# Spreading the roundings of weight sums, a later free time for five buffers, and separate banks for the last product

## The chip, the cores and the metric

The kernel runs on one core of one Trainium2 chip. The metric is the device time of one launch in microseconds (us), as the median of several runs; lower is better. A core has TensorE (PE, matmuls), VectorE (DVE), ScalarE (ACT), GpSimd (POOL) and SyncE (SP); here SP issues nearly all DMA transfers.

## The reference

Sigmoid attention, then a feed-forward layer with squared ReLU:

```python
S = q.shape[2]                                   # q, k, v: (8, 12, 448, 64)
scores = np.matmul(q, k.transpose(0, 1, 3, 2)) / np.sqrt(64) - np.log(S)
attn = np.matmul(1.0 / (1.0 + np.exp(-scores)), v)
x = attn.transpose(0, 2, 1, 3).reshape(3584, 768)
h = x @ w_in                                     # (768, 2048)
r = np.maximum(h, 0.0)
out = (s * (r * r) + b) @ w_out                  # (2048, 768)
```

All in float32. The kernel keeps the precision by splitting a float32 operand into a high part (rounded to the matmul format fp32r) and a low part (the difference), and by three matmuls for each product: high by high, high by low, low by high (`PARTS`).

## The kernel before

**Attention (0 to 246 us of the trace).** 8 batches by 12 heads are done in 24 steps, "quads" of four heads. In each step TensorE makes the scores (L812, L833) and the product with v (L845, L853), ScalarE the sigmoid (L788), VectorE the split of q and k. What these engines have left goes to the weights of the feed-forward layer. `convert` turns a block of stored weights into the form that is needed (integer and float steps on VectorE and ScalarE, L659 to L677), `sums_out` (L913) makes sums and differences of blocks of the second weight matrix for the fast scheme below. A group g of sums is made (`make`, VectorE), its high part is rounded (`hi`, ScalarE, L930), its low part is a subtraction on VectorE (`lo`), and SP stores it to DRAM. In which step each of the three is done stands in the table `SUMS_AT`: for f = 0 and 1 three rows, for `make`, `hi` and `lo`, with seven groups each. `at_step` puts a function into a step's list of an engine.

**Plain stage (246 to 371 us).** The first 512 tokens go through the two matrices in the ordinary way, in 16 blocks of the 2048 inner columns: `ffn1` (L981) fills a PSUM bank ph_f, ScalarE empties it into r_f (L1505) and makes g_f from it, VectorE makes the low part of g_f, and `ffn2` (L1374) multiplies it into po. The weights w_l_f of matrix l, block f, are split here: high part on ScalarE (`base_hi`, L694), low part on VectorE (`base_lo`, L638 by `sub`).

**Fast scheme (371 to 972 us).** The other 3072 tokens, in two groups of three blocks of 512, use a scheme that multiplies sums of blocks (`LAYERS`). One layer has 29 products, each in two halves p of 12 matmuls of 512 columns, 0.22 us apart. Layer 0 makes h from operands s, layer 1 the output from operands g. An operand of product r in layer 0 of group n is s`n`_`r`_0h (high part, ScalarE L1145) and s`n`_`r`_0l (low part, VectorE L638). Weight sums wu come by DMA from DRAM. During layer 0 of the first group `later_sums` (L1286) makes the last weight sums t_*: VectorE adds, ScalarE rounds (L1348), VectorE subtracts (low part), SP stores to DRAM (L1354) and then the buffer is free again.

**The order of the work.** From the plain stage on, all work is first listed as operations with an engine, a cost, a due time and what they need. `Flow.run` (L227) then simulates the engines and fixes, engine by engine, the order in which they are written out. An operation can also need a buffer. Buffers are kept by `Slots` (L561), a list sorted by the time since when each is free; `tile` takes the first of that list, `free` puts one back with the planner's time. `cx.more(t2, 5, "t")` (L1061) adds five buffers that lie over the attention's memory. The planner's start time of an operation is not before its buffer's free time:

```python
def more(self, pl, n, tag, old=None):
    self.free_ += [(pl, f"{tag}{i}", old(i) if old else 0.0) for i in range(n)]
    self.free_.sort(key=lambda x: x[2])
...
key = (max(at, o.ready, o.heap.ready(need)), o.due)
```

The order within an engine is fixed once it is written; where an instruction uses a buffer whose last reader is on another engine or in a DMA, it waits for that one on the chip.

**The end.** `build` (L430) lists the products. The last product (number 20 of layer 1 in the second group) writes three parts of an output block into banks of its second half, and `last_out` adds them to C1_20, which goes out in three stores.

## Time and profile before

| | us |
|---|---|
| median of 3 runs | 977.67 |
| lowest, highest | 976.95, 978.43 |
| the profiled execution | 977.93 |
| its span in the trace | 976.1 |
| TensorE busy in it | 970.9 |
| VectorE busy | 875.8 |
| ScalarE busy | 719.8 |

All times of the trace count from the start of the span. An instruction's row gives its start and duration; on VectorE and ScalarE successive rows overlap by a little under 0.1 us. Idle time before an instruction stands in brackets with what ended it. TensorE's granted clock was 1.00 over the span.

### The profile page before, as it was taken

What the parts mean: (1) busy time and instruction counts of PE and PEld (TensorE: products, weight loads), DVE (VectorE), ACT (ScalarE), POOL (GpSimd) and SP (SyncE); (2) the same over time, 40 slices, a digit from 0 to 9 for tenths busy, and PEclk for the clock granted to TensorE, in tenths of its full rate; (3) what the DMA queues carried; (4) which work ended last, traced back from release to release, by engine and by line L of the source; (5) the groups of instructions that cost most, each with busy time, mean ns of one, the idle gap of its engine ahead of it and who ended that gap; (6) DMA issues with size and microseconds to landing.
All of it is one profiled execution on the core that took longest, in us unless ns stands there. A gap on an engine that the chain in (4) does not pass through costs nothing.

```text
span 976.1 us, 13892 instructions
## 1 busy us (share of the span) xinstructions
PE 970.9 (99%) x5192; PEld 764.8 (78%) x5192; DVE 875.8 (90%) x995; ACT 719.8 (74%) x807; POOL 0.2 (0%) x4
## 2 busy tenths in 40 slices
PE   9999999999999999999999999999999999999998
PEld 4555545555788888888888888888888888888887
DVE  5998999999899988899999999999787649999995
ACT  7999999999777767557799996333457499995330
POOL 0000000000000000000000000000000000000000
PEclk9999999999999999999999999999999999999999
DMA  8789999998569999989986666799866666666675
GB/s 327 286 308 350 326 364 401 351 396 311 191 263 365 354 403 413 414 279 320 341 287 206 202 203 205 226 333 330 311 201 202 207 200 207 200 205 202 201 251 194
DMA packets 97377, 276.68 MB, mean 283 GB/s; under 512 B 10016, under 2 KB 23456, under 8 KB 97312
## 3 DMA queue, kind: packets, MB, share of 16 engines
q1 hardware_dynamic: 97024, 275.35, 81.2%
q8 instruction: 41, 0.67, 0.3%
q10 hardware_dynamic: 288, 0.46, 0.1%
q14 instruction: 24, 0.20, 0.1%
HBM read 193.99 MB, written 81.79 MB: 283 GB/s over the span
## 4 chain that ended last, share of the span: by engine, by line
PE 97%; ACT 1%; DVE 1%; issue 0%; DMA 0%; DVEq 0%; ACTq 0%
PE o L1166 30%; PE h L1166 27%; PE pav L845 11%; PE psc L812 7%; PE po L1374 6%; PE ph L981 6%; PE e L1166 4%; PE psc_l L833 2%; PE pav L853 2%; PE pav L812 1%; DVE C L635 0%; ACT a L788 0%; PE idle L873 0%; DMA xd<-xo 0%; ACT w L694 0%
## 5 line engine op out<-in xcount | busy, mean ns | idle before, releaser
L1166 PE MATMUL h<-s_0h,wu 128*128 128x512 f32 x800 | 239.2, 379 | 0.0
L1166 PEld LDWEIGHTS h<-s_0h,wu 128*128 128x128 f32 x800 | 151.2, 189 | 21.5
L1166 PE MATMUL h<-s_0l,wu 128*128 128x512 f32 x400 | 151.6, 379 | 0.0
L1166 PE MATMUL o<-g_0h,wu 128*128 128x512 f32 x464 | 147.5, 379 | 0.0
L1166 PE MATMUL o<-g_1h,wu 128*128 128x512 f32 x456 | 144.9, 379 | 0.0
L788 ACT ACTIVATE a<-psc,nls 128x896 f32<-128x896 f32 x120 | 113.7, 1027 | 10.4 <-PE psc L812 8.3
L845 PE MATMUL pav<-a,v 128*64 128x448 f32 x576 | 113.8, 543 | 0.0
L1166 PEld LDWEIGHTS o<-g_0h,wu 128*128 128x128 f32 x464 | 87.7, 189 | 12.4
L1166 PEld LDWEIGHTS o<-g_1h,wu 128*128 128x128 f32 x456 | 86.2, 189 | 12.2
L845 PEld LDWEIGHTS pav<-a,v 128*64 128x64 f32 x576 | 39.1, 137 | 62.7 <-issue 56.0
L1166 PE MATMUL o<-g_0l,wu 128*128 128x512 f32 x232 | 87.9, 379 | 0.0
L1166 PE MATMUL o<-g_1l,wu 128*128 128x512 f32 x228 | 86.4, 379 | 0.0
L1166 PEld LDWEIGHTS h<-s_0l,wu 128*128 128x128 f32 x400 | 75.6, 189 | 10.7
L1258 ACT ACTIVATE G<-G 128x1024 f32<-128x1024 f32 x56 | 57.7, 1049 | 27.2 <-DVE G L638 13.6
L1374 PE MATMUL po<-g,w 128*128 128x512 f32 x288 | 64.4, 379 | 0.0
L1374 PEld LDWEIGHTS po<-g,w 128*128 128x128 f32 x288 | 54.4, 189 | 7.7
L981 PE MATMUL ph<-x0h,w 128*128 128x512 f32 x192 | 59.8, 380 | 0.3 <-ACT r L1505 0.3
L1128 ACT COPY G<-h 128x1024 f32<-128x1024 f32 x36 | 36.0, 1013 | 29.1 <-PE h L1166 28.3
L638 DVE TENSOR_TENSOR qkl<-qk,qkh 128x1664 fp32r<-128x1664 f32 (+3 forms) x26 | 44.9, 1726 | 13.9 <-ACT qkh L767 13.6
L1258 ACT ACTIVATE G<-G,b_sb,s_sb 128x1024 f32<-128x1024 f32 x40 | 49.0, 1235 | 0.1
L1166 PEld LDWEIGHTS o<-g_0l,wu 128*128 128x128 f32 x232 | 43.8, 189 | 6.2
L1166 PEld LDWEIGHTS o<-g_1l,wu 128*128 128x128 f32 x228 | 43.1, 189 | 6.1
(195 smaller groups left out, 1908.0 us busy)
## 6 DMA issues: line engine op xcount, KB each, us to landing
wu<-wd SPq DMA_DIRECT2D x232, 512.0 KB, 4.4
wd<-t SPq DMA_DIRECT2D x42, 768.0 KB, 7.5
qk<-qk_t SPq DMA_DIRECT2D x23, 896.0 KB, 7.4
st<-w_out SPq DMA_DIRECT2D x16, 768.0 KB, 8.8
st<-w_in SPq DMA_DIRECT2D x16, 768.0 KB, 9.2
v<-v_t SPq DMA_DIRECT2D x24, 448.0 KB, 5.7
xd<-xo SPq DMA_DIRECT2D x24, 448.0 KB, 4.3
out_t<-C SPq DMA_DIRECT2D x17, 512.0 KB, 5.0
```

The costliest lines, as they stand in the source:

```text
L638: nc.vector.tensor_tensor(o, x, y, op=ALU.subtract)
L788: nc.scalar.activation(a, psc[:, :, :S], AF.Sigmoid, bias=nls, scale=SCALE)
L812: nc.tensor.matmul(o[j][:, :S], two[wi][r, i, cols], paired(two[xi][r, i, :S]), start=m == 0, stop=m == 2,)
L833: nc.tensor.matmul(spread(psc[half[i], j, :S]), x[r, i, 1, 3 * P :], x[r, i, 0, :], start=True, stop=True,)
L845: nc.tensor.matmul(pav[i][r, :S], ld_[1][:, 3 * i + c, j, :], a[i, c][:, j, :], start=c == 0, stop=False,)
L853: nc.tensor.matmul(pav[i][r, :S], ld_[1][half[i], 6, j, :], a[half[i], j, :], start=False, stop=True,)
L981: nc.tensor.matmul(ph, w[:, k, wi, kc * P : (kc + 1) * P], paired(x0[h][xi][:, cc, :]), start=m == 0, stop=m == 3 * NCC - 1,)
L1128: nc.scalar.copy(o, self.view(x, l))
L1166: nc.tensor.matmul(bank.t[0][:, j], wt[:, w, wi, x * P : (x + 1) * P], paired((o.hi, o.lo)[xi][:, c, :]), start=new and m == 0, stop=stop ...
L1258: v.by = flow.op("ACT", cost, lambda: nc.scalar.activation(f32(v.t), f32(v.t), *a, **kw), (v.by,))
L1374: nc.tensor.matmul(pos[e], w[:, k, wi, kc * P : (kc + 1) * P], paired(g[:, gi, :]), start=first and i == 0, stop=last and i == 2,)
```

## The change

Three edits.

1. `SUMS_AT` and `sums_out`: a step has at most one rounding of sums on ScalarE. Before, steps 11, 16 and 21 had two. Three of the 14 roundings go to VectorE as a cast (steps 10, 18 and 20, written as negative numbers); one low part moves from step 18 to 19; the last sum of one group moves from step 5 to 6.
2. The five t2 buffers count as free at 5.0 of the planner's time, not 0.0. The planner's decisions in the plain stage and in layer 0 of the first group come out otherwise, from that stage on.
3. The last product uses the banks of the two lanes that are not busy with the product before it; the addition of an earlier partial result to C1_20 is listed by itself and can run before the last product. Its first half runs 6 matmuls of 512 columns and 12 of 256 in place of 12 of 512.

```diff
--- before.py
+++ after.py
@@ -41,8 +41,8 @@
 PIECES = (2, 1, 1, 2, 1, 1, 2, 1, 1, 2, 1, 1, 2, 1, 1, 2, 1, 1, 2, 1, 2, 1)
 LATE, LATE_AT, LATE_FOR = 2, 2, 5
 SUMS_AT = (
-    ((3, 4, 5, 7, 8, 9, 11), (4, 5, 7, 8, 10, 11, 11), (6, 6, 9, 9, 11, 12, 13)),
-    ((12, 14, 15, 16, 17, 19, 21), (14, 16, 16, 17, 19, 21, 21), (15, 17, 18, 18, 21, 22, 22)),
+    ((3, 4, (5, 5, 5, 5, 6), 7, 8, 9, 11), (4, 5, 7, 8, -10, 10, 11), (6, 6, 9, 9, 11, 12, 13)),
+    ((12, 14, 15, 16, 17, 19, 21), (14, 16, -18, 17, 19, -20, 21), (15, 17, 19, 18, 21, 22, 22)),
 )
 
 
@@ -476,17 +476,20 @@
                     tag = 2 * lane + p if l == 0 else lane
                     new = r in fresh and (l == 0 or p == 0)
                     if l == 0 or p == 0:
-                        bank = Bank(tag, l, None if new else last[tag])
-                        waits = last[tag].readers if tag in last else []
+                        b_was = last.get(tag)
+                        bank = Bank(tag, l, None if new else b_was)
+                        waits = b_was.readers if b_was else []
                         last[tag] = bank
                     else:
                         bank, waits = last[tag], []
                     stop = l == 0 or p == np_ - 1
-                    final_unit = l and end and x == len(seq) - 1 and p == np_ - 1
-                    if final_unit:
-                        part = net.join(*rest[0], Val(u, 1, bank), s_last, f"C{n}_e", True)
+                    final_unit = l and end and x == len(seq) - 1
+                    if final_unit and p == 0:
+                        assert not new and seq[-2][1] != lane
+                        part = net.join(*rest[0], Val(b_was.by, 1, b_was), s_last, f"C{n}_e", True)
                         part.name = k_last
-                        waits = [q for t, b in last.items() if t != tag for q in b.readers]
+                        tags = sorted((t for t in last if t != seq[-2][1]), key=lambda t: t == tag)
+                        waits = [q for t in tags for q in (b_was if t == tag else last[t]).readers]
 
                     ended = None
                     seeds = r in L["seeds"] and not (l and end and x == len(seq) - 1)
@@ -500,7 +503,7 @@
 
                     def fn(n=n, l=l, r=r, p=p, o=o, bank=bank, new=new, stop=stop, final_unit=final_unit):
                         if final_unit:
-                            em.last(n, r, p, o, bank.tag)
+                            em.last(n, r, p, o, tags, p == 0, stop)
                         else:
                             em.unit(n, l, r, p, o, bank, new, stop)
                         o.uses -= 1
@@ -509,8 +512,9 @@
                             flow.heap.free(o.lo)
 
                     u = em.matmuls(flow, net.UNIT, fn, [o.by, *waits], n, l, r, p)
-                    if final_unit:
+                    if final_unit and stop:
                         flow.op("DVE", 2.0, lambda: em.last_out(n, part, s_last), (u, part.by))
+                    bank.by = u
                     if stop and ended:
                         v = Val(u, 1, bank)
                         if l == 0:
@@ -926,8 +930,8 @@
             at[n] = f32(ts[g][:, k, here])
             op(at[n], get(x), sign, get(y))
 
-        def hi(g):
-            nc.scalar.copy(ts[g][:, :, 0], f32(ts[g][:, :, 1]))
+        def hi(g, copy=nc.scalar.copy):
+            copy(ts[g][:, :, 0], f32(ts[g][:, :, 1]))
 
         def lo(g):
             t = ts[g]
@@ -948,9 +952,13 @@
         made_at = collections.Counter()
         for g, (n, h, low) in enumerate(zip(*steps)):
             for i in range(len(SUMS[g])):
-                at_step(n, "DVE", 3.05 + 0.1 * made_at[n] if n > 3 else 4, lambda g=g, i=i: make(g, i))
-                made_at[n] += 1
-            at_step(h, "ACT", 2, lambda g=g: hi(g))
+                m = n[i] if isinstance(n, tuple) else n
+                at_step(m, "DVE", 3.05 + 0.1 * made_at[m] if m > 3 else 4, lambda g=g, i=i: make(g, i))
+                made_at[m] += 1
+            if h > 0:
+                at_step(h, "ACT", 2, lambda g=g: hi(g))
+            else:
+                at_step(-h, "DVE", 3.3, lambda g=g: hi(g, nc.vector.tensor_copy))
             at_step(low, "DVE", 3.25, lambda g=g: lo(g))
 
     pieces = [(l, f + h * (NF // 4)) for f in range(NF // 4) for l in (1, 0) for h in (0, 2, 1, 3)]
@@ -1058,7 +1066,7 @@
     rt, p2, gp = Slots(rt_pool, 2, "r"), Slots(p2_pool, 3, "w"), Slots(gp_pool, 3, "g")
     ps_o = pool(blk_ps, "ps_o", 1, space=PSUM)
     t2 = pool(blk, "t2", 1)
-    cx.more(t2, 5, "t")
+    cx.more(t2, 5, "t", lambda i: 5.0)
     wfp_late = pool(blk, "wfp_late", 1)
     for _, f in late:
         wf_tile(0, f, wfp_late)
@@ -1171,21 +1179,22 @@
                         )
                         m += 1
 
-        def last(self, n, r, p, o, busy):
+        def last(self, n, r, p, o, tags, new, stop):
             wt = fetched[stream.index((n, 1, r, p))]
-            tags = [x for x in range(4) if x != busy]
-            self.ends = []
-            for e, tk in LAST:
-                b = ps.tile([P, 2, TB], F32, tag=f"b{tags.pop(0)}", name=f"o_{e}_{tk.start}")[:, 0, tk]
+            if new:
+                self.ends = [
+                    ps.tile([P, 2, TB], F32, tag=f"b{t}", name=f"o_{e}_{tk.start}")[:, 0, tk]
+                    for t, (e, tk) in zip(tags, LAST)
+                ]
+            for (e, tk), b in zip(LAST, self.ends):
                 q = 0
                 for f in range(2):
                     for wi, gi in PARTS:
                         nc.tensor.matmul(
                             b, wt[:, f, wi, e * P : (e + 1) * P], paired((o.hi, o.lo)[gi][:, f, tk]),
-                            start=q == 0, stop=q == 5, skip_group_check=True,
+                            start=new and q == 0, stop=stop and q == 5, skip_group_check=True,
                         )
                         q += 1
-                self.ends.append(b)
 
         def last_out(self, n, part, sign):
             m, k = self.block[part.name]
```

Most of what moves follows from the second edit and can't be seen in the diff. Rows are in program order of an engine; what stands behind "waits" are the semaphores of the engine (or DMA ring) that the instruction waits for. The change's lines are 4 to 9 higher for the same code (L642 is L638 before).

First place: VectorE at the start of the plain stage. Names are w_l_f for weights (matrix l, block f), wf_f and st_f for a weight block that `convert` still works on and the load that it comes from. Before:

```order
L638 TENSOR_TENSOR w_0_1_2773<-wf_0_1_101,w_0_1_2773 128x3x256 [waits DMAHW2_49,DMAHW6_49,DMAHW1_49,Activation_49]
L638 TENSOR_TENSOR w_1_0_2775<-wf_1_0_96,w_1_0_2775 128x3x256 [waits Activation_49]
L638 TENSOR_TENSOR w_0_9_2778<-wf_0_9_103,w_0_9_2778 128x3x256 [waits Activation_49]
L638 TENSOR_TENSOR w_1_8_2802<-wf_1_8_98,w_1_8_2802 128x3x256 [waits Activation_49]
L659 TENSOR_SCALAR wf_0_7_2740<-st_0_7_2769 128x768 [waits DMAHW7_49]
L659 TENSOR_SCALAR wf_0_15_2741<-st_0_15_2771 128x768 [waits DMAHW0_49]
```

With the change:

```order
L642 TENSOR_TENSOR w_0_8_2748<-wf_0_8_99,w_0_8_2748 128x3x256 [waits Activation_49]
L642 TENSOR_TENSOR w_1_0_2773<-wf_1_0_96,w_1_0_2773 128x3x256 [waits Activation_49]
L663 TENSOR_SCALAR wf_0_7_2740<-st_0_7_2769 128x768 [waits DMAHW7_49]
L642 TENSOR_TENSOR w_0_1_2778<-wf_0_1_101,w_0_1_2778 128x3x256 [waits DMAHW5_49,Activation_49]
L642 TENSOR_TENSOR t_0_0_0_2807<-wf_0_4_113,wf_0_12_115 128x256 [waits DMAHW2_49,DMAHW1_49]
L642 TENSOR_TENSOR w_0_9_2804<-wf_0_9_103,w_0_9_2804 128x3x256 [waits DMAHW6_49,DMAHW2_49,Activation_49]
```

The integer step on wf_0_7, which waits for the load of st_0_7 (DMAHW7), stood behind the low parts of w_0_1, w_1_0, w_0_9 and w_1_8, and stands now ahead of those of w_0_1, w_0_9 and w_1_8. TensorE's next block, ph_1, uses w_0_1.

Second place: VectorE in layer 0 of the first group, where TensorE does products 21, 19 and 1. s0_19_0l is the low part of product 19's operand; t_t4, t_t6, t_t11, t_t13 are weight sums; G00_13 and G01_13 are joins of results. Before:

```order
L638 TENSOR_TENSOR t_t13_4326<-t_t13_4326 128x2x256 [waits DVE_49,Activation_49]
L638 TENSOR_TENSOR t_t4_4432<-wr_4_4025,t_t4_4432 128x2x256 [waits DVE_49]
L638 TENSOR_TENSOR s0_19_0l_4454<-a_0_01_3901,s0_19_0h_4403 128x1024 [waits Activation_49]
L635 TENSOR_TENSOR t_t6_4470<-wr_5_3999,t_t4_4432 128x2x256 [waits DVE_49,PE_49]
L638 TENSOR_TENSOR t_t3_4345<-t_t3_4345 128x2x256
L635 TENSOR_TENSOR t_t11_4477<-wr_4_4025,t_t6_4470 128x2x256 [waits DVE_49]
L638 TENSOR_TENSOR t_t4_4432<-t_t4_4432 128x2x256 [waits Activation_49]
L635 TENSOR_TENSOR a0_t7_4307<-a_0_00_4068,a0_t7_4307 128x1024
L638 TENSOR_TENSOR G00_13_4203<-G00_13_4203,h_0_13_0_4214 128x1024 [waits PE_49]
L638 TENSOR_TENSOR t_o26_4503<-t_t8_4412,t_t11_4477 128x2x256 [waits DVE_49,PE_49]
L638 TENSOR_TENSOR s0_1_0l_4521<-a_0_02_4071,s0_1_0h_4499 128x1024 [waits DMAHW6_49,Activation_49]
```

With the change:

```order
L642 TENSOR_TENSOR t_t13_4327<-t_t13_4327 128x2x256 [waits DVE_49,Activation_49]
L642 TENSOR_TENSOR t_t4_4445<-wr_4_4023,t_t4_4445 128x2x256 [waits DVE_49]
L642 TENSOR_TENSOR a_0_02_4071<-a_0_02_4071,a_0_12_3572 128x1024
L639 TENSOR_TENSOR t_t6_4470<-wr_5_3997,t_t4_4445 128x2x256 [waits DVE_49,PE_49]
L642 TENSOR_TENSOR t_t3_4347<-t_t3_4347 128x2x256 [waits Activation_49]
L639 TENSOR_TENSOR a0_t7_4308<-a_0_00_4068,a0_t7_4308 128x1024
L642 TENSOR_TENSOR G00_13_4202<-G00_13_4202,h_0_13_0_4212 128x1024 [waits Activation_49]
L642 TENSOR_TENSOR t_t4_4445<-t_t4_4445 128x2x256 [waits DVE_49]
L639 TENSOR_TENSOR t_t11_4498<-wr_4_4023,t_t6_4470 128x2x256 [waits PE_49]
L642 TENSOR_TENSOR G01_13_4231<-G01_13_4231,h_0_13_1_4236 128x1024 [waits Activation_49]
L642 TENSOR_TENSOR s0_19_0l_4511<-a_0_01_3901,s0_19_0h_4401 128x1024 [waits DMAHW0_49,DVE_49]
L642 TENSOR_TENSOR t_o26_4514<-t_t8_4425,t_t11_4498 128x2x256 [waits DVE_49]
```

s0_19_0l was two rows behind the low part of t_t13 and waited for ScalarE alone. It is now three rows behind the low part of t_t4 and waits for a DMA (DMAHW0): the store of t_t4 to DRAM, whose buffer it takes. G00_13 ahead of it waits for a copy by ScalarE. The low part s0_1_0l, eight rows behind s0_19_0l before and now seven (outside these rows), waits with the change for TensorE's end of product 19, from which it takes a buffer, and before for a store's landing.

Third place: the rows of ScalarE that the second place waits for, with the change:

```order
L1357 CAST t_t6_4470<-t_t6_4470 128x2x256 [waits DVE_49]
L1136 COPY G00_12_4493<-h_0_13_0_4212 128x1024 [waits DMAHW4_49,PE_49]
L1267 ACTIVATE G00_t1_4123<-G00_t1_4123,b_sb_79,s_sb_78 128x1024 [waits Activation_49]
L1136 COPY G01_12_4501<-h_0_13_1_4236 128x1024 [waits PE_49]
L1155 ACTIVATE s0_24_0h_4506<-a_0_21_3611 128x1024 [waits DMAHW6_49,DVE_49]
```

G00_12 waits for the landing of the store of t_t13 (DMAHW4), whose buffer it takes, and for TensorE.

## Rows read from the trace of the kernel before

**Rows 1.** The page, part 1: engine, busy us, share of the span, instructions.

```profile
PE 970.9 (99%) x5192; PEld 764.8 (78%) x5192; DVE 875.8 (90%) x995; ACT 719.8 (74%) x807; POOL 0.2 (0%) x4
```

**Rows 2.** TensorE's waits over the whole program: us in total, times, longest.

```profile
PE ph L981 <- ACT r L1505: 0.3, 1, 0.3
```

**Rows 3.** Windows of three quads: us, busy by engine, clock, DMA share.

```profile
66.11:76.28 10.17, 10.17 (x81) 5.39 (x78) 9.13 (x12) 9.59 (x12) 0.00 (x0) 1.00 0.88 289
126.21:136.41 10.20, 10.20 (x81) 5.31 (x78) 9.90 (x16) 10.20 (x13) 0.00 (x0) 1.00 1.01 396
206.50:216.50 10.00, 10.00 (x80) 5.39 (x76) 8.97 (x12) 9.59 (x12) 0.00 (x0) 1.00 1.04 407
```

**Rows 4.** Timeline of ScalarE, 120 to 127 us: start, duration, engine, line, operation.

```profile
124.97 1.59 ACT L930 CAST t<-t 128x768 fp32r<-128x768 f32 x2
126.43 1.04 ACT L788 ACTIVATE a_l<-psc_l,nls 128x896 f32<-128x896 f32 x1
```

**Rows 5.** Timeline of VectorE at 240.5 us: a cast of 128x768.

```profile
240.53 0.94 DVE L694 CAST w<-wf 128x768 fp32r<-128x768 f32 x1
```

**Rows 6.** Timeline of ScalarE, 246 to 256 us.

```profile
250.71 3.03 ACT L694 CAST w<-wf 128x768 fp32r<-128x768 f32 x4 [5.33 <-DMA xd<-xo]
```

**Rows 7.** Timeline of TensorE, 253.5 to 258.5 us.

```profile
253.59 0.38 PE L981 MATMUL ph<-x0h,w 128*128 128x512 f32 x1
254.29 0.48 PE L981 MATMUL ph<-x0h,w 128*128 128x512 f32 x1 [0.32 <-ACT r L1505]
...
258.28 2.97 PE L1374 MATMUL po<-g,w 128*128 128x512 f32 x13
```

**Rows 8.** Timeline of VectorE, 246 to 261 us.

```profile
251.57 3.56 DVE L638 TENSOR_TENSOR w<-wf,w 128x768 fp32r<-128x768 f32 x4 [3.21 <-ACT w L694]
255.05 0.71 DVE L659 TENSOR_SCALAR wf<-st 128x768 int32<-128x768 int32 x1
256.17 0.68 DVE L659 TENSOR_SCALAR wf<-st 128x768 int32<-128x768 int32 x1 [0.41 <-DMA st<-w_in]
256.76 0.42 DVE L638 TENSOR_TENSOR t<-wf,wf 128x256 f32<-128x256 f32 x1
```

**Rows 9.** SP from 246 us, and its DMA to landing, 247.9 to 248.1.

```profile
247.94 1.61 SPq L1400 DMA_DIRECT2D st<-w_in  x2
...
st<-w_in SPq DMA_DIRECT2D x1, 768.0 KB, 6.1
```

**Rows 10.** Timeline of VectorE, 434 to 444 us.

```profile
436.15 0.68 DVE L638 TENSOR_TENSOR t_t<-t_t 128x512 fp32r<-128x512 f32 x1
...
437.35 1.22 DVE L638 TENSOR_TENSOR s_0l<-a,s_0h 128x1024 fp32r<-128x1024 f32 x1
```

**Rows 11.** Timelines of SP and of ScalarE, 436 to 443 us.

```profile
436.86 0.32 SPq L1354 DMA_DIRECT2D wd<-t_t  x1
...
442.41 1.05 ACT L1145 CAST s_0h<-a 128x1024 fp32r<-128x1024 f32 x1 [1.04 <-DMA wd<-t_t]
```

**Rows 12.** Us to landing: stores at 436.86, at 446.82, all of 424-452.

```profile
wd<-t_t SPq DMA_DIRECT2D x1, 512.0 KB, 5.5
...
wd<-t_t SPq DMA_DIRECT2D x1, 512.0 KB, 4.4
...
DMA to landing us min/median/max: 3.3/5.0/6.7
```

**Rows 13.** Timeline of TensorE at 443.7 us.

```profile
443.68 0.38 PE L1166 MATMUL h<-s_0l,wu 128*128 128x512 f32 x1
```

**Rows 14.** Timeline of TensorE, 0 to 6 us.

```profile
0.77 3.15 PE L873 MATMUL idle<-const-bfloat16-1.0 128*128 128x448 bf16 x8 [0.77 <-PEq L1638]
```

**Rows 15.** Timeline of VectorE, 960 to 977 us.

```profile
966.84 1.22 DVE L635 TENSOR_TENSOR C_t<-C_t,o 128x1024 f32<-128x1024 f32 x1 [2.77 <-PE o L1166]
...
970.37 2.67 DVE L635 TENSOR_TENSOR C<-C,o 128x1024 f32<-128x1024 f32 x4
```

**Rows 16.** Timeline of TensorE, 969 to 977 us, its last row.

```profile
971.75 0.28 PE L1183 MATMUL o<-g_1h,wu 128*128 128x256 f32 x1
```


## The prediction

> **What bounds the kernel now.** I read the busy times first, then TensorE's waits, then the stretches where its work is spread wider than elsewhere, and only there the other engines. TensorE is busy 970.9 of 976.1 us [rows 1], and its waits hold one short entry after the start, 0.3 us for a ScalarE result [rows 2]. So no VectorE, ScalarE or DMA time that is saved can show in the end, except where TensorE is held up today: four stretched quads of the attention, one point at the start of the plain stage, and the work behind its last matmul. What can show everywhere is the reverse: an operand that comes late. The change rewrites the order on VectorE, ScalarE and SP, which are in-order, so I went through its order for instructions that now stand behind a wait and have TensorE waiting for them.
>
> **Base of the sum.** The profiled execution took 977.93 us (span 976.1 and 1.83 around it), 0.26 over the median of 977.67. The terms are added to 977.93.
>
> **Attention.** Roundings spread out: -0.80. An undisturbed quad lasts 9.99 to 10.00 us, as the one at 206.50; the one at 66.11 lasts 10.17 and the one at 126.21 lasts 10.20 [rows 3]; the pattern of the latter comes twice more, at 176.35 and 226.50. Ahead of the one at 126.21 ScalarE ran two roundings of sums in a row (124.97, 1.59 us), and the sigmoid on which the quad depends began at 126.43, after TensorE's quad had begun [rows 4]. The change leaves one such rounding a step, so three times 0.21 goes, and with the last sum of step 5 moved to step 6 the 0.17 at 66.11: 0.80 in all. The three roundings now on VectorE cost it about 0.94 each, by the cast of the same size [rows 5]; the quad at 206.50 has 10.00 - 8.97 = 1.03 us of VectorE idle [rows 3], so it fits, barely. If it did not, up to 0.3 us of each gain would come back; bounds -0.8 to 0.
>
> **Plain stage.** At its start, +1.65. Today four casts of weights on ScalarE wait 5.33 us for the landing of the attention's last store, start at 250.71 [rows 6], and delay the ScalarE result that empties TensorE's bank: TensorE starts a matmul at 254.29 that was due 0.22 (one matmul's pitch) after 253.59 [rows 7]. That 0.48 goes, since ScalarE's order now has the first weight cast free of that store: -0.5. In its place VectorE has got a new wait. The low part of weight piece w_0_1 stood ahead of the integer step on wf_0_7; it now stands right behind it, and that step waits for the load st_0_7. Today that load is the first of two issued at 247.94, takes 6.1 us to land [rows 9], so 254.03, and VectorE, with the step one place behind four such low parts, starts it at 255.05 [rows 8] without a wait. After the change VectorE stands until 254.03, runs the step (0.71) and the low part (3.56 / 4 = 0.89), and is done at 255.64. TensorE wants that operand with the third matmul of its group; without today's delay the group begins at 253.81, the third matmul at 254.24. Lost: 1.45 with the semaphore. The queue behind is late as well: a 0.42 subtraction, a low part 0.89, the step on wf_0_15 (0.68; today it starts at 256.17, when its load lands, and here about then too), a low part 0.89, three small operations of 0.42 [rows 8], then g_0's low part, 0.68 as other subtractions of 128x512 [rows 10]. End to end, with the overlap of about 0.08 that successive rows show, that ends near 260.0; the first product of the second matrix [rows 7] needs it at 258.28 + 0.22 - 0.48 + 1.45 = 259.4: another 0.7. Net -0.5 + 1.45 + 0.7 = +1.65; bounds -0.5 (the load lands early) to +2.5 (the load lands 1 us later).
>
> **Product 19.** In layer 0 of the first group, +6.8. The planner took the five t2 buffers as free at 0.0; with 5.0 they go to the end of its list of free places, so the tiles rotate through other buffers. The low part s0_19_0l waited for ScalarE alone, ran at 437.35, and TensorE used it at 443.68 [rows 10, 13]. In the new order it takes the place of the sum t_t4, so it needs that sum stored to DRAM first, and the chain to it is serial: VectorE finishes t_t13 as today, 436.15 + 0.68, and the store is issued at 436.86 and lands 5.5 us later [rows 10, 11, 12]. ScalarE's copy G00_12, which has taken t_t13's place, waits for that landing (today another ScalarE instruction waits for the same landing and starts at 442.41 [rows 11]) and takes about as long as that row, 1.05: 443.46. VectorE's queue stands at G00_13, which needs the copy: 1.22, to 444.68. Behind it, only now, t_t4's low part: 0.68, to 445.36. Then the store and its landing, then s0_19_0l, 1.22. For the landing of such stores between 424 and 452 us the trace has from 3.3 to 6.7 us, and 4.4 for the one issued at 446.82 [rows 12]. The shortest was issued ahead of a load into an idle queue, as the new one will be if the load before it has landed; the one of 4.4 had a load ahead of it. I take the middle of the two, 3.9. VectorE then ends at 445.36 + 3.9 + 1.22 = 450.5, and TensorE, which wants it at 443.68, stands 6.8 us. Bounds: 5.0 where t_t13 also lands in 3.3 us (then the copy follows TensorE's own product at about 441.2) and 9.6 with 6.7. The Trainium skill, DMA: Bandwidth & Descriptors, "Anatomy of one DMA", puts a transfer at about 2.0 us plus its bytes over 436 GB/s; for 512 KB that would be 3.2 us, near the 3.3 of rows 12, and by it this term would be 6.1.
>
> **Product 1.** Next in order, +1.27. The low part s0_1_0l used to take a buffer that a store freed. It now takes the place of an operand of product 19 and can begin only after that product's last matmul. TensorE's first matmul of product 1 has its operand, the second waits for 1.22 of VectorE and two semaphores of 0.05; 1.27 after the pitch. This one has no cover and no spread; its bounds are 1.0 and 1.5.
>
> **Clock.** After the stall, +1.6. No stretch of the trace has TensorE idle for microseconds in mid-program, so the price is bounded. Nothing: 0. The nearest row with an idle TensorE before it is the program's start: eight matmuls of 448 columns take 3.15 us there [rows 14], 0.37 us from start to start, which is the 1.2 GHz level; at 2.4 GHz they would take half, so 1.6 us were lost. Twice that, 3.2, is my upper end. I take 1.6. The Trainium skill, TensorE: Matmul & The Clock Gate, "What's actually happening", says that the default state is the throttled one and that activity releases it; rows 14 agree for the start, and no row here shows a fall later.
>
> **Last product.** In banks of its own, -0.55. Today VectorE takes in C_t1 at 966.84, after 2.77 us of idle, two joins, then at 970.37 four additions for 2.67 us, to 973.04 [rows 15], while TensorE's last matmul ends at 971.75 + 0.28 = 972.03 [rows 16]. The first of the four needs nothing of the last product and now runs in that idle time. The end then follows TensorE: 972.03 + 0.05 for six more starts of short matmuls, a semaphore, and the last addition of 0.41, 972.49: 0.55 earlier. Bounds -0.3 to -0.6. The stores behind it move along.
>
> **Sum.** 977.93 - 0.80 + 1.65 + 6.8 + 1.27 + 1.6 - 0.55 = 987.9 us.
>
> **Rivals.**
> 1. The clock stays at its high level. For: it was granted in full in every stretch that I looked at [rows 3]. Against: rows 14. Then 987.9 - 1.6 = 986.3.
> 2. The big stall is covered: t_t13 lands early and the store of t_t4 gets through at once, or VectorE is ahead of where I put it, so that TensorE sees almost nothing of product 19 and 1. For: today's order has 5 us of slack at this place, from 438.57 to 443.68 [rows 10, 13]. Against: three steps in series with two landings between them. Then 977.93 - 0.80 + 1.65 - 0.55 = 978.2, no change.
> 3. Not slower: nothing new is waited for at all, st_0_7 included. It decides at whether the loads and stores land before VectorE comes to the waits, that is st_0_7 by 252 and t_t4 by 442. Then only the gains stay: 977.93 - 0.80 - 0.5 - 0.55 = 976.1, at the edge of what is told from no change. Against: st_0_7 landed at 254.03, and t_t4's place in the row is behind a copy that TensorE itself releases near 441.
> 4. VectorE overruns in the attention and the late landings pile up (6.7 us in the big stall): 987.9 + 0.8 + 2.8 = 991.5.
>
> **How the numbers follow.** Forecast with the clock's loss 0.68, rival 1 0.15, rival 2 0.07, rival 3 0.05, rival 4 0.05. The low end takes rival 1 with the big stall at its lower bound, 5.0, and the plain stage near +0.2: 983.0; the high end stops at rival 4, 991.5. What is told from no change is 0.2%, 1.95 us around 977.67: 975.7 to 979.6. Rival 2 lies inside, rival 3 mostly; faster 0.02, same 0.10, slower 0.88.
>
> **What would show it.** TensorE's waits should list two large new entries in layer 0 of the first group: some 7 us for VectorE's s0_19_0l, with VectorE's idle before it ended by the landing of a wd<-t_t store, and 1.3 us for s0_1_0l. Near 254 a wait of about 1.4 us for VectorE's w, ended by st<-w_in on VectorE. The quads from 66 to 236 us should all last 10.0. After the stall the matmuls should be 0.43 apart for a few microseconds if the clock falls. VectorE's end should follow TensorE's last matmul by 0.5 us. No wait over 2 us in layer 0 would prove me wrong.

## The result, and the profile after

The changed kernel takes 988.22 us (median of 4, 987.60 to 989.33) against 977.87 for the kernel before in the same runs: ratio 1.0104, 95% interval 1.0092 to 1.0117. Forecast were 987.9 us and slower, range 983.0 to 991.5. The profiled execution is the longest of the four, 989.33 us with a span of 987.25, 11.1 over the 976.14 before.

TensorE's waits, over the whole program of the changed kernel (us in total, times, longest), against the single short one of [rows 2]:

```profile
PE h L1174 <- DVE s_0l L642: 6.6, 2, 5.5
PE ph L989 <- DVE w L642: 1.2, 1, 1.2
PE idle L877 <- PEq L1647: 0.8, 1, 0.8
PE po L1383 <- DVE g L642: 0.7, 1, 0.7
```

The idle matmul's wait of 0.8 stood there before as well. The other three are new, and each names VectorE: s_0l for products 19 and 1, w at the start of the plain stage, g behind it. To see what each cost, I took the start of every matmul in the new trace less that of the same matmul in the trace before:

| stretch | the difference goes from, to (us) | cost | forecast |
|---|---|---|---|
| program start, to 8 us | 0 to +0.33 | +0.3 | 0 |
| attention | +0.33 to -0.22 | -0.55 | -0.80 |
| start of the plain stage | -0.22 to +1.64 | +1.9 | +1.65 |
| product 19, the wait | +1.64 to +7.28 | +5.6 | +6.8 |
| the 13 matmuls behind it | +7.28 to +10.2 | +2.9 | +1.6 |
| product 1 | +10.2 to +11.6 | +1.4 | +1.27 |
| from there to the last matmul | +11.6 to +11.6 | 0 | 0 |
| VectorE's last result behind it | 1.01 to 0.46 | -0.55 | -0.55 |

Before rounding the rows add up to +11.1, all that the span grew by. A single trace carries all of these readings; the other three executions are 1 to 2 us shorter than the profiled one.

**Attention.** Windows of the new trace: a quad that is now undisturbed ahead of one that is not, a second such one, and the clock in layer 0 (us, busy time of PE, PEld, DVE, ACT, POOL, then granted clock, DMA share, GB/s):

```profile
116.38:126.37 9.99, 9.99 (x80) 5.39 (x77) 9.88 (x14) 9.59 (x12) 0.00 (x0) 1.00 0.89 326
126.37:136.48 10.11, 10.11 (x81) 5.39 (x77) 9.86 (x16) 9.59 (x12) 0.00 (x0) 1.00 1.02 381
186.41:196.53 10.12, 10.12 (x81) 5.39 (x77) 8.79 (x12) 9.59 (x12) 0.00 (x0) 1.00 1.00 377
...
450.90:457.10 6.20, 6.15 (x15) 4.94 (x16) 3.64 (x5) 1.84 (x3) 0.00 (x0) 0.53 0.47 175
457.10:459.10 2.00, 2.00 (x10) 1.51 (x8) 1.35 (x3) 0.27 (x1) 0.00 (x0) 1.00 0.85 201
```

The quad that lasted 10.20 [rows 3] lasts 10.11. VectorE was busy 9.88 of the 9.99 us ahead of it. The quad at 186.41, which lasted 9.99 before, now lasts 10.12; VectorE was busy 9.91 of the 10.01 us ahead of that one.

**Plain stage.** VectorE in the new trace (start, us, and in brackets the idle time before and what ended it), where [rows 8] had four low parts in one go at 251.57:

```profile
253.93 0.58 DVE L663 TENSOR_SCALAR wf<-st 128x768 int32<-128x768 int32 x1 [4.91 <-DMA st<-w_in]
254.43 0.93 DVE L642 TENSOR_TENSOR w<-wf,w 128x768 fp32r<-128x768 f32 x1
...
256.78 0.71 DVE L663 TENSOR_SCALAR wf<-st 128x768 int32<-128x768 int32 x1 [0.22 <-DMA st<-w_in]
257.37 0.99 DVE L642 TENSOR_TENSOR w<-wf,w 128x768 fp32r<-128x768 f32 x1
...
259.24 0.73 DVE L642 TENSOR_TENSOR g<-r,g 128x512 fp32r<-128x512 f32 x1
```

VectorE stands 4.91 us for the load st_0_7, then does the step on wf_0_7, and the second row is the low part of w_0_1 that TensorE waits for. The last row is g_0's low part. TensorE there, to be held against [rows 7]:

```profile
255.42 0.70 PE L989 MATMUL ph<-x0h,w 128*128 128x512 f32 x2 [1.24 <-DVE w L642]
...
260.02 2.21 PE L1383 MATMUL po<-g,w 128*128 128x512 f32 x9 [0.67 <-DVE g L642]
```

**Layer 0.** The serial chain, engine by engine. ScalarE's timeline: the copy G00_12, released by the landing of t_t13's store:

```profile
443.77 1.01 ACT L1136 COPY G<-h 128x1024 f32<-128x1024 f32 x1 [0.65 <-DMA wd<-t_t]
```

VectorE's timeline: G00_13, which waited for that copy; t_t4's low part; s0_19_0l, which waited for the landing of t_t4's store; further on s0_1_0l, which waited for TensorE:

```profile
444.81 1.22 DVE L642 TENSOR_TENSOR G<-G,h 128x1024 f32<-128x1024 f32 x1 [1.92 <-ACT G L1136]
445.95 0.69 DVE L642 TENSOR_TENSOR t_t<-t_t 128x512 fp32r<-128x512 f32 x1
...
449.67 1.23 DVE L642 TENSOR_TENSOR s_0l<-a,s_0h 128x1024 fp32r<-128x1024 f32 x1 [1.30 <-DMA wd<-t_t]
...
459.05 1.23 DVE L642 TENSOR_TENSOR s_0l<-a,s_0h 128x1024 fp32r<-128x1024 f32 x1 [0.65 <-PE h L1174]
```

SP's timeline: its last issue before, the store of t_t4, and the load behind it:

```profile
442.70 0.32 SPq L1091 DMA_DIRECT2D wu<-wd  x1
446.70 0.32 SPq L1363 DMA_DIRECT2D wd<-t_t  x1
447.12 0.38 SPq L1091 DMA_DIRECT2D wu<-wd  x1
```

That store's time to landing, from the DMA part of the trace at 446.7 us:

```profile
wd<-t_t SPq DMA_DIRECT2D x1, 512.0 KB, 2.9
```

TensorE's timeline; it had product 19's first matmul behind it and stood until s0_19_0l was there:

```profile
450.95 0.79 PE L1174 MATMUL h<-s_0l,wu 128*128 128x512 f32 x1 [5.48 <-DVE s_0l L642]
451.54 1.06 PE L1174 MATMUL h<-s_0h,wu 128*128 128x512 f32 x2
...
457.12 0.38 PE L1174 MATMUL h<-s_0l,wu 128*128 128x512 f32 x1
...
460.33 0.48 PE L1174 MATMUL h<-s_0l,wu 128*128 128x512 f32 x1 [1.10 <-DVE s_0l L642]
```

Behind the first matmul of this stretch, at 450.95, they are 0.43 apart, from 457.12 on 0.22. The windows above say the same: 0.53 granted between 450.90 and 457.10, which is 1.2 GHz for nearly all of it, and 1.00 behind.

**The end.** VectorE, against [rows 15]; TensorE's last matmul starts at 983.37 and takes 0.28:

```profile
975.56 1.22 DVE L639 TENSOR_TENSOR C<-C,o 128x1024 f32<-128x1024 f32 x1
978.42 1.22 DVE L639 TENSOR_TENSOR C_t<-C_t,o 128x1024 f32<-128x1024 f32 x1 [1.64 <-PE o L1174]
...
982.35 1.09 DVE L639 TENSOR_TENSOR C<-C,o 128x512 f32<-128x512 f32 x2 [0.31 <-PE o L1193]
983.68 0.42 DVE L639 TENSOR_TENSOR C<-C,o 128x256 f32<-128x256 f32 x1 [0.25 <-PE o L1193]
```

The first row is the addition to C1_20, now ahead of C_t. VectorE ends at 984.10, 0.46 after TensorE.

### The profile page after: what moved, and what is told of

It is laid out like the page before. It is cut to its first block, busy times and chain, and to the rows that moved or that the text cites. A ratio compares the mean times of both kernels' runs of the same rounds, so it can differ in the third digit from the quotient of the medians.

```text
span 987.3 us, 13920 instructions
## 1 busy us (share of the span) xinstructions
PE 974.4 (99%) x5198; PEld 767.5 (78%) x5198; DVE 879.0 (89%) x998; ACT 718.6 (73%) x804; POOL 0.2 (0%) x4
## 4 chain that ended last, share of the span: by engine, by line
PE 94%; DVE 2%; DMA 2%; ACT 1%; issue 1%; SPq 0%; ACTq 0%; DVEq 0%
PE o L1174 30%; PE h L1174 24%; PE pav L849 11%; PE psc L816 7%; PE po L1383 6%; PE ph L989 5%; PE e L1174 4%; PE psc_l L837 2%; PE pav L857 2%; PE pav L816 1%; DMA wd<-t_t 1%; DMA st<-w_in 1%; DVE G L639 1%; PE o L1193 1%; DVE s_0l L642 0%
## 5 line engine op out<-in xcount | busy, mean ns | idle before, releaser
L1174 PE MATMUL o<-g_0h,wu 128*128 128x512 f32 x456 | 144.9, 379 | 0.0
L642 DVE TENSOR_TENSOR qkl<-qk,qkh 128x1664 fp32r<-128x1664 f32 (+3 forms) x26 | 44.9, 1726 | 11.9 <-ACT qkh L771 11.4
```

Of the source, the lines that this page charges most:

```text
L642: nc.vector.tensor_tensor(o, x, y, op=ALU.subtract)
L1174: nc.tensor.matmul(bank.t[0][:, j], wt[:, w, wi, x * P : (x + 1) * P], paired((o.hi, o.lo)[xi][:, c, :]), start=new and m == 0, stop=stop ...
```

## The experiments

The theory: the whole loss comes from the second edit, in two places that have nothing to do with each other, and in each a VectorE instruction now stands behind a transfer (product 1, behind the second place, waits for TensorE itself). The rivals: the first edit has a part in it, since it moves stores; the slow matmuls behind the wait are something other than the clock; any later free time does the same harm. Each run was timed in turn with the kernel before on the same chip; "TensorE" numbers are starts of matmuls less those of the trace before, as in the table.

**The second edit undone (e1_no_late).**

```diff
-    cx.more(t2, 5, "t", lambda i: 5.0)
+    cx.more(t2, 5, "t")
```

> The changed kernel with the five t2 buffers free from 0.0 again (second edit undone, first and third kept). Theory: the whole loss comes from the second edit, so its waits (0.6 at w_0_1, then 1.2 and 0.7 in the plain stage, 5.5 and 1.1 in layer 0) and the 2.9 us of slow matmuls go, and the gains of the other two edits stay: 977.9 - 0.55 (attention) - 0.4 (end) = about 976.9, between 976.3 and 977.5, ratio to before 0.999. Rival: the first edit, by moving the stores of the sums, takes part in the late landings; then some of the plain stage's waits stay and the time is over 978.5.

Measured: 977.03 us, ratio 0.9993 (0.9984 to 1.0001). None of the three waits is left; TensorE's waits are those of the kernel before, the 0.3 for ScalarE at 254 us included (0.6 with what follows it). In the trace the first and the third edit give 0.3 in the attention and 0.55 at the end, together under 0.1%, which the runs can't tell from nothing.

**The second edit alone (e2_only_late)**, in the kernel before, the same line.

> The kernel before with the second edit alone. Theory: all waits of the changed kernel are there and none of its gains: 988.2 + 0.55 + 0.4 = about 989.2, 988 to 990.5. Rival: the waits need the first edit's later stores as well; then the plain stage's 1.9 us are missing and the time is 987 or less.

Measured: 989.53 us, ratio 1.0121 (1.0108 to 1.0135). All of TensorE's waits are there:

```profile
PE h L1166 <- DVE s_0l L638: 6.8, 2, 5.7
PE ph L981 <- DVE w L638: 1.2, 1, 1.2
...
PE po L1374 <- DVE g L638: 0.6, 1, 0.6
```

TensorE is 0.28 late at 250 us and 11.75 late at the end. The other two edits are not needed for any of it; the rival that gives the first edit a part falls.

**The third edit alone (e3_only_last).**

> The kernel before with the third edit alone. Theory: -0.4 us by what the traces show at the end (before: VectorE's last addition ends 1.0 after TensorE's last matmul; changed: 0.45 after), so 977.4. Rival: the longer first half (12 short matmuls in place of 6) and the stores behind eat it, then no change.

Measured: 977.75 us, ratio 0.9997 (0.9987 to 1.0006), not to be told from no change. In the trace VectorE's last result comes 0.46 us after TensorE's last matmul, 1.01 before: the term is there, and too small for the runs.

**The first edit alone (e5_only_sums).**

> The kernel before with the first edit alone. Theory: the quads at 66, 126, 176 and 226 us lose part of what they had over 9.99; by the changed kernel's trace -0.55 us in all (predicted were -0.80, two quads keep 0.12 each because VectorE is full in the step ahead), so 977.9 - 0.55 = 977.3 and TensorE about 0.5 earlier at 250 us than at 30 us. Rival: the gain needs the third edit or is lost in the plain stage; then TensorE's lead at 400 us is back to 0.

Measured: 977.75 us, ratio 0.9994 (0.9985 to 1.0002). TensorE's difference goes from -0.30 at 8 us to -0.77 at 250 us: -0.47, and none of it is lost later.

**The wait filled with work (e4_dummies).** To find out what the slow matmuls are, TensorE gets matmuls of zeros into the running sum, ahead of the second matmul of product 19; `zeros` lies in memory that was only padding and is set to zero by GpSimd, `wide` is a constant operand of ones.

```diff
+    zeros = pool(ctx, "pad", 1, side="right").tile([P, 112], BF16, tag="pad", name="pad")
+    nc.gpsimd.memset(zeros, 0.0)
...
+    wide = ones
...
+                        if (n, l, r, p, j, m) == (0, 0, 19, 0, 0, 1):
+                            for _ in range(24):
+                                nc.tensor.matmul(
+                                    bank.t[0][:112, j], zeros, wide, start=False, stop=False, skip_group_check=True
+                                )
```

> The changed kernel with 24 more matmuls of zeros (112 columns of weights, 512 columns, adding nothing to the sum) between the first and the second matmul of product 19, so that TensorE works through most of its longest wait. Theory: the 14 slow matmuls after the wait (0.43 apart) are the lower clock after idle time; with the wait filled they are 0.22 apart and the time falls by 2.9 us, to about 985.3; the waits themselves stay (24 x 0.22 = 5.2 of the 5.5 us are work now). Rival: they are slow for another reason (late weights or operands), then nothing changes, 988.2.

Measured: 986.17 us, ratio 1.0089 (1.0075 to 1.0103). TensorE at this place:

```profile
444.52 5.39 PE L1178 MATMUL h<-const-bfloat16-1.0,pad 128*112 128x512 bf16 x24
450.10 0.48 PE L1181 MATMUL h<-s_0l,wu 128*128 128x512 f32 x1 [0.19 <-DVE s_0l L643]
450.42 0.59 PE L1181 MATMUL h<-s_0h,wu 128*128 128x512 f32 x2
```

Of TensorE's wait 0.19 us are left, its delay stays: the difference still rises by 5.6 us at this matmul. But in the 13 matmuls behind it, it rises by 0.1 and not by 2.9; they are 0.22 apart, and the granted clock from 450.0 to 453.5 is 1.00. VectorE still ends s0_19_0l only 0.06 us before the matmul. So all but 0.1 of the 2.9 us are the clock, and idle time brought it down. The median is 0.9 over the 985.3 expected, the profiled execution (985.74) 0.4; in this trace the plain stage cost 1.1 us and not 1.9, since st_0_7 landed 1.1 us sooner after its issue, so totals alone would not have separated the two.

**Half as many (e6_dummies12)**, 12 in place of 24.

> As the run with 24 matmuls of zeros, with 12: TensorE then works 2.6 us of its long wait and stands for some 2.9. Theory, weakly held, since waits of 1.2 us in the plain stage left the clock full: 2.9 us are not enough for the lower level either, matmuls after the wait 0.22 apart, time near 986. Rival: what counts is any idle time of some microseconds; then the 2.9 us of slow matmuls come back, in part or whole, and the time is 987.5 to 988.5.

Measured: 989.42 us (four executions of 988.0 to 990.45), ratio 1.0113 (1.0100 to 1.0126). My weak guess was wrong: TensorE stood 3.18 us, and the clock had fallen.

```profile
444.64 2.77 PE L1178 MATMUL h<-const-bfloat16-1.0,pad 128*112 128x512 bf16 x12
450.59 0.58 PE L1181 MATMUL h<-s_0l,wu 128*128 128x512 f32 x1 [3.18 <-DVE s_0l L643]
450.97 1.06 PE L1181 MATMUL h<-s_0h,wu 128*128 128x512 f32 x2
...
454.32 0.38 PE L1181 MATMUL h<-s_0l,wu 128*128 128x512 f32 x1
```

Windows of the same trace, with the columns of the windows above:

```profile
450.50:454.30 3.80, 3.71 (x9) 2.95 (x10) 2.62 (x5) 1.89 (x3) 0.00 (x0) 0.55 0.38 154
454.30:457.00 2.70, 2.70 (x14) 2.35 (x13) 2.04 (x2) 0.00 (x0) 0.00 (x0) 1.00 0.82 220
```

The slow matmuls end at 454.3, after 1.8 us of loss and not 2.9. By that the time should be some 1 us below that of the changed kernel. The profiled execution is (988.0); the median isn't. The other three were not traced. The mean granted clock is 0.998 in the profiled execution and in the one of 988.91, but 0.996 in those of 989.93 and 990.45, against 0.996 and 0.997 in the changed kernel: by that those two spent longer at the lower clock than the trace shows; why stays open.

**8.0 in place of 5.0 (e8_eight).**

> The changed kernel with 8.0 in place of 5.0. Its order has the step on wf_0_7 ahead of the low part of w_0_1 as with 5.0, but s0_19_0l waits for ScalarE alone and s0_1_0l for a store as before the change. Theory: the two places are independent; the plain stage loses its 1.9 us and layer 0 nothing, clock included: 977.9 - 0.4 + 1.9 - 0.45 = 978.9. Rival: any later free time makes layer 0 lose; then 985 or more.

Measured: 979.46 us, ratio 1.0014 (1.0005 to 1.0023). TensorE's waits:

```profile
PE ph L989 <- DVE w L642: 1.1, 1, 1.1
PE po L1383 <- DVE g L642: 1.1, 1, 1.1
PE idle L877 <- PEq L1647: 0.8, 1, 0.8
...
```

The plain stage costs +2.3 here (-0.36 to +1.94), layer 0 nothing, and the mean granted clock of the traced execution is 1.00 (one other, of 981.78 us, has 0.998 and was not traced). The two places are independent, and a later free time as such does no harm in layer 0; the rotation of the buffers that 5.0 happens to give does.

**Two loads planned as if they moved 2000 KB (e7_slow_loads, e10_again).** The 5.0 stays. The planner then takes the two late weight loads, st_0_7 and its like, to last 7.6 us in place of 4.5; the data are the same.

```diff
-            o = do("SP", 0.1, load, need=1, kb=768)
+            o = do("SP", 0.1, load, need=1, kb=2000)
```

> The changed kernel, 5.0 kept, with one number changed: the planner is told that the two late weight loads (st_0_7 and its like) take 2000 KB's time in place of 768, that is 7.6 us and not 4.5, where the trace has 6.1 and 7.5. The data moved are the same. Theory: the loss is not in the buffers' free time as such but in an order that rests on landings that are planned too early. Then VectorE takes the low parts of w_0_1, w_0_9 and w_1_8 ahead of the step on wf_0_7, the plain stage's waits of 1.2 and 0.7 go and its gain of 0.6 stays, and in layer 0 s0_19_0l and s0_1_0l get buffers that no late store holds: 977.9 - 0.4 - 0.6 - 0.45 = 976.4, faster than both. Rival: the 5.0 alone makes the waits in layer 0; then TensorE still waits some 5 us there and the time is about 986.

> The kernel with slow loads told to the planner, once more and unchanged, since two of its 12 executions took 1128 and 2642 us. Theory: 976.4 again and no such execution, they belonged to the machine. Rival: they belong to the kernel and come again.

Measured: 976.40 us, ratio 0.9980 (0.9971 to 0.9989), and again 976.28, ratio 0.9983 (0.9974 to 0.9991). Two of the first run's 12 executions took 1128 and 2642 us, none of the second's 11; what made those two long stays open. TensorE waits for nobody after the start:

```profile
PE idle L877 <- PEq L1647: 0.8, 1, 0.8
```

VectorE's timeline at the plain stage has the low parts ahead of the step on wf_0_7 (254.10), which no longer waits; s0_19_0l runs at 436.27 without a wait:

```profile
250.48 0.96 DVE L642 TENSOR_TENSOR w<-wf,w 128x768 fp32r<-128x768 f32 x1 [1.75 <-ACT w L698]
...
252.03 0.95 DVE L642 TENSOR_TENSOR w<-wf,w 128x768 fp32r<-128x768 f32 x1
...
253.23 0.95 DVE L642 TENSOR_TENSOR w<-wf,w 128x768 fp32r<-128x768 f32 x1
254.10 0.70 DVE L663 TENSOR_SCALAR wf<-st 128x768 int32<-128x768 int32 x1
...
436.27 1.22 DVE L642 TENSOR_TENSOR s_0l<-a,s_0h 128x1024 fp32r<-128x1024 f32 x1
```

All three gains of the change are there in the trace (0.6 in the attention, 0.6 in the plain stage, 0.55 at the end), and this kernel is 0.2% faster than the one before and 1.2% faster than the changed one.

**Every landing planned at 4.0 us in place of 2.5 (e11_landing).**

```diff
-    FAR, LATENCY, RATE, LANDING = 8.0, 0.2, 390.0, 2.5
+    FAR, LATENCY, RATE, LANDING = 8.0, 0.2, 390.0, 4.0
```

> The changed kernel, 5.0 kept, with the planner's landing time of every DMA at 4.0 us and not 2.5. Theory: as with the slow loads, orders that rest on early landings go: the low part of w_0_1 comes ahead of the step on wf_0_7, and s0_19_0l no longer waits for a store, but it takes the place of an operand of the product before, so that TensorE waits the fixed 1.2 us for it and the clock stays full: 977.9 - 0.4 - 0.6 + 1.2 + 0.3 (g_0's low part behind the step on wf_0_15) - 0.45 = 978.0. Rival: layer 0 keeps the long wait; 984 or more.

Measured: 979.63 us, ratio 1.0018 (1.0009 to 1.0027). The long wait is gone and the short fixed one is in its place, as expected; not expected was a wait for a weight load at 373 us. SP issues that load at 362.77, behind two stores that stood after it in the changed kernel, and it landed after 10.1 us:

```profile
PE h L1174 <- DVE s_0l L642: 1.3, 1, 1.3
...
PE h L1174 <- DMA wu<-wd: 0.7, 1, 0.7
```

A wait of 1.3 us left the clock at 1.00 in this trace. The median is 1.6 over what I expected: TensorE's difference rises by 0.9 at the load and by 1.6 at s0_19_0l, where I had 1.2, and the median is 1.0 over the profiled execution (978.62). Two of the 11 executions, of 982.45 and 983.01 us, have a mean granted clock of 0.998; they were not traced. A number closer to the truth does not by itself give a better plan: every number reshuffles the buffers.

**Three low parts a step later (e9_lo_later)**, on top of the slow loads.

```diff
-    ... (6, 6, 9, 9, 11, 12, 13)),
+    ... (6, 6, 9, 9, 12, 13, 13)),
-    ... (15, 17, 19, 18, 21, 22, 22)),
+    ... (15, 18, 19, 18, 21, 22, 22)),
```

> The kernel with slow loads told to the planner, and with three low parts of sums one step later (f = 0: steps 11 and 12 to 12 and 13; f = 1: 17 to 18). Theory: the quads at 126 and 186 us last 10.1 because VectorE has no idle time in the step ahead (0.10 and 0.10 us) and the second pair of matmuls waits for its low part; with 0.9 us taken out of those two steps all quads last 9.99, TensorE is 0.22 ahead at 250 us, and the time is 976.2, not to be told from 976.4 by the runs. Rival: the stores of these sums, a step later, hold buffers of later loads, and a quad further on loses as much.

Measured: 976.33 us, ratio 0.9985 (0.9976 to 0.9994): by the runs, not to be told from the kernel without it. By the trace the two quads have lost their 0.12 each; windows of three quads:

```profile
116.27:126.26 9.99, 9.99 (x80) 5.39 (x76) 9.36 (x14) 9.59 (x12) 0.00 (x0) 1.00 0.94 355
126.26:136.25 9.99, 9.99 (x80) 5.39 (x76) 9.70 (x16) 9.60 (x12) 0.00 (x0) 1.00 0.91 295
186.20:196.19 9.99, 9.99 (x82) 5.39 (x78) 9.56 (x12) 9.60 (x12) 0.00 (x0) 1.00 0.90 297
```

All quads last 9.99, and TensorE's difference goes from +0.22 at 8 us to -0.58 at 250 us, the -0.80 of the forecast.

## Why the prediction was right, point by point

**The mechanism** held in every step of the loss, and the edit that I held responsible is the one (e1_no_late, e2_only_late). Of the signs that I had named, one did not come: the quads do not all last 10.0 us. The order of the changed kernel alone showed where TensorE would stand; the trace of before gave the durations.

**Plain stage: +1.65 forecast, +1.9 measured.** The load landed at 253.90 (254.03 before), the low part of w_0_1 followed as worked out, 254.43 + 0.93. The second part of the term was 0.9 and not 0.7, and the step on wf_0_15 had to wait 0.22 for its own load; my 0.7 was itself a slip, since 258.28 + 0.22 - 0.48 + 1.45 is 259.47, and 260.0 with a semaphore of 0.05 less that is 0.6. The whole term hangs on the load's landing: in e4_dummies, e6_dummies12 and e2_only_late, with the same order, it landed 5.1, 5.8 and 6.1 us after its issue, 6.2 here, and the stage cost 1.1, 1.7, 1.7 and 1.9.

**Product 19: +6.8 forecast, +5.6 measured; this term was mis-sized.** The chain is the forecast one, in its order. TensorE was 1.64 late when it came to it; without that the copy started at 443.77 - 1.64 = 442.13 (forecast 442.41), the store went out at 445.06 (445.36). But the store landed after 2.9 us and I had put 3.9, between two stores of before of 3.3 and 4.4 [rows 12]. That is 1.0 of the 1.2.

It is no chance of one execution: the same store landed after 2.9 us in the traces of e2_only_late, e4_dummies and e6_dummies12 as well. SP had issued nothing for 4.0 us before it, since 442.70. In the traces of before and after (424 to 453 us), the stores that SP issued within 1.7 us of its issue ahead took 4.2 to 6.7 us to land. Those issued 2.5 and 3.2 us behind it took 3.3 and 4.4, those issued 4.0 and 5.3 us behind it 2.9 and 2.6. So the free time ahead goes with the landing, though no run set out to test it; the prediction named the idle queue and took the middle of two landings even so. The Trainium skill, DMA: Bandwidth & Descriptors, "Anatomy of one DMA", has about 2.0 us plus the bytes over 436 GB/s as a fit to transfers that GpSimd issues; worked out for this store, which SP issues, that is an estimate of 3.2 us, and the trace comes out 0.3 lower.

**The clock: +1.6 forecast, +2.9 measured; mis-sized as well.** I took the only stretch of slow matmuls that the trace of before had, eight of 448 columns, and gave twice its loss as the upper end. That stretch follows the start of the program, not a wait, so nothing in it said how long TensorE stays slow behind one; the 1.6 was a guess within bounds, and 2.9 lies near the upper one. (The profile's granted clock reads 1.00 even there, from 0 to 4.5 us; that those eight ran at the 1.2 GHz level is read from their pitch, 0.37 us against 0.19 for the 448 columns of the attention.) The loss differs from trace to trace: 2.5 in e2_only_late, behind a wait of 5.66. That the clock fell is shown by the granted 0.53, and e4_dummies shows that the idle time did it. The Trainium skill, TensorE: Matmul & The Clock Gate, "What's actually happening", has the array fall back to 1.2 GHz when it has been idle, and the trace agrees. The rival without it (986.3) is refuted.

**Product 1: +1.27 forecast, +1.4 measured**, without cover as said; 460.33 follows the end of VectorE's 459.05 + 1.23 by 0.05.

**Attention: -0.80 forecast, -0.55 measured.** I took VectorE's room from the quad at 206.50 with 1.03 us of idle. The steps that decide were the two ahead of the quads at 126 and 186; in the first 9.99 - 9.88 = 0.11 us were left, in the second 0.10. I had said "barely" and gone on with the full gain; e9_lo_later shows that it is to be had. The 0.3 us that I let come back of each gain has no row behind it and is more than the gain of such a quad, 0.21.

**The end: -0.55 forecast and measured.**

So the forecast of 987.9 is nearer to the 988.22 than its terms are to theirs: -1.2 on the store and +1.3 on the clock cancel, and that is luck. Against the profiled execution, from which the terms are read, the sum of terms was +10.0 and came out +11.1.

**The rivals.** Rival 2 (covered) and 3 (nothing waited for) needed the landings early; they weren't. Of rival 4 VectorE's overrun in the attention came, with a third of its price, and the long landing didn't. Rival 3's mirror exists all the same: with a plan in which VectorE never stands behind those transfers, the gains alone remain, 976.3 to 976.4 (e10_again, e7_slow_loads) against the 976.1 worked out for it.

## What to carry to other kernels

Where a planner writes in-order queues, the damage of a small change is read from the order, not from the diff: look for instructions that now stand behind a wait and have the bounding engine waiting for something further down the same queue. A chain that goes to memory and back before an operand may be written costs its landing times in series, and if it stops TensorE for microseconds, the matmuls behind run at half speed for a while: here waits of 3.2 to 5.7 us cost 1.8 to 2.9 us more, about half the price again. When a planned order rests on a transfer landing in time, hold its planned landing against the landing times in the trace before touching anything else, and re-read the order after every such correction.

## What the runs showed of the hardware that I had not expected

- After a wait of 5.48 us TensorE ran 13 matmuls at the 1.2 GHz level, 0.43 apart, and lost 2.9 us by it; after one of 5.66 us it lost 2.5 (e2_only_late), after one of 3.18 us 1.8 (e6_dummies12), each in the traced execution. After waits of 1.24, 0.67 and 1.10 us (changed kernel) and of 1.3 us (e11_landing) the matmuls were 0.22 apart from the second on, with a first gap of 0.32. With the long wait filled by matmuls of zeros the clock stayed at 1.00 (e4_dummies).
- Stores of 512 KB to DRAM landed after 2.6 to 6.7 us in the same stretch of the program, 424 to 453 us (traces of before and after). The one on which product 19 waits landed after 2.9 us in four traces.
- The first microseconds differ from run to run: TensorE's start of the attention was between 0.3 us earlier and 0.75 us later than in the trace before, in kernels that are the same up to there. Differences under 0.2% are read inside the trace, from stretch to stretch, not from the totals.
